# Linear attention and a SwiGLU block in one kernel: one more turn by DMA, wider slots, an earlier q load, and four banks for the last y

**Chip, cores, metric.** One core of one Trainium2 chip. The metric is the device time of one launch in microseconds (us). The device time is about 1.8 us longer than the span that the profile shows. Positions such as 36.29 are us from the start of the span.

## The reference, cut to what matters

```
k_proj = einsum('ks,bhsd->bhkd', E, k);  v_proj = einsum('ks,bhsd->bhkd', F, v)
attn   = softmax(q @ k_proj^T / 8)                 # 8 batches, 8 heads, 1024 tokens, 64 x 64
x      = (attn @ v_proj), heads side by side       # 8192 tokens x 512
g = x @ w_gate;  val = x @ w_val                   # 512 -> 1536
out = (g * sigmoid(g) * val) @ w_out               # 1536 -> 512, float32
```

## The kernel before

The kernel walks over 16 chunks of 512 tokens (two per batch) and, in each, over 12 blocks of 128 features. A block is four gate matmuls (`gps`), four value matmuls (`vps`) and, for the chunk before, four matmuls of the output (`yps`), each 512 columns wide. The attention of later tokens is placed between them in numbered slots: slot 2t lies between gate and value of block t, slot 2t+1 after value and output. The attention of one quarter of a half batch is called a unit: q is turned (`u_T`: four TensorE transposes, then a copy from PSUM), scores and exponential follow (`u_S`), then row sums (`u_R`, VectorE), normalisation (`u_N`, GpSimd), the turn of the attention (`u_A`: four transposes and a copy), and the product with v (`u_PV`, copied to xT, which the next chunk's matmuls read). In the profile `qTp`, `sc`, `aTp` and `pv` are the four results in PSUM, and `qT`, `ee` (the exponential), `AT` and `xT` what is made of them in SBUF; `qTd` and `AAd` belong to the turns by DMA.

```python
def u_T(b, u, at="a", eng=nc.scalar):          # turn of q by TensorE
    ps = bank(at, [P, 4, P], BF16, "qTp")
    for n in range(4):
        nc.tensor.transpose(out=ps[:, n, :], in_=..., identity=ident_bf[:])
    copy(eng, t[:], ps[:])                     # 128 x 512 bf16
def u_TD(b, ch):                               # the same for half a batch by DMA
    nc.sync.dma_start_transpose(out=t[:], in_=qb[b, ch]...)
def u_A(b, u, eng=nc.vector): ...              # turn of attention by TensorE; u_AD by DMA
def u_PV(b, ch, pr, eng=nc.scalar): ...        # one 512-column matmul, copied to xT
# (cut)
def f_y(c, n):
    if part == 0:
        if c == B * CH - 1 and i % 2: yy[c] = ps_g.tile(...)   # a gps bank
        else:                         yy[c] = ps_y.tile(...)   # the one y bank
    # 4 of 12 accumulating matmuls; after the last: ScalarE copy, store from SyncE's queue
# (cut) batch 0, second half
for i, u in enumerate(range(4, 8)):
    put(14+i, u_T, 0, u); put(15+i, u_S, 0, u); put(16+i, u_R, 0, u)
    put(16+i, u_N, 0, u); put(19+i, u_A, 0, u)
put(22, u_PV, 0, 1, 0); put(22, u_PV, 0, 1, 1); put(23, u_PV, 0, 1, 2); put(23, u_PV, 0, 1, 3)
```

Batches 2 to 7 are turned by DMA, batches 0 and 1 by TensorE. The products, turns and scores share three PSUM banks.

The softmax here doesn't subtract the row's maximum and nothing guards it: scores larger than these inputs give would overflow.

Of the kernel before, what the change touches and what calls it, by code (L numbers as in the profile page):

```python
# [9 lines left out]
AF = mybir.ActivationFunctionType  # L10
# [3 lines left out]
FP32 = mybir.dt.float32  # L14

B = 8
H = 8
S = 1024
D = 64
KP = 64  # L20
DM = H * D
DFF = 1536
P = 128
NJ = S // P
NPAIR = H // 2
NKT = DM // P
NFT = DFF // P
CH = 2
CW = 512
NIT = B * CH * NFT  # L30
BY_DMA = range(2, B)


@with_exitstack
def kernel(
# [19 lines left out]
    nc = tc.nc  # L55
    scale = 1.0 / float(D) ** 0.5
# [9 lines left out]
    y_pool = ctx.enter_context(tc.tile_pool(name="ysb", bufs=3))  # L66
    ps_g = ctx.enter_context(tc.tile_pool(name="psg", bufs=2, space=bass.MemoryType.PSUM))
    ps_v = ctx.enter_context(tc.tile_pool(name="psv", bufs=2, space=bass.MemoryType.PSUM))
    ps_y = ctx.enter_context(tc.tile_pool(name="psy", bufs=1, space=bass.MemoryType.PSUM))
# [11 lines left out]
    wo = w_pool.tile([P, NFT, DM], BF16, name="wo")  # L81
# [20 lines left out]
    def load_q(b, ch, parts=1):  # L102
        t = q_pool.tile([P, H, 4, D], BF16, name="qb", tag="qb")
        qb[b, ch] = t
        n = H // parts
        for i in range(parts):
            nc.gpsimd.dma_start(
                out=t[:, i * n : (i + 1) * n].rearrange("p h j d -> p h (j d)"),
                in_=q[b, i * n : (i + 1) * n].rearrange("h (p c j) d -> p c h (j d)", c=2, j=4)[:, ch],
            )  # L110

    def load_w_gv(c0, c1, which=(0, 1)):
        cs = slice(c0 * P, c1 * P)
        for wsrc, wdst in [((moe_w_gate, wg), (moe_w_val, wv))[i] for i in which]:
            nc.gpsimd.dma_start(
                out=wdst[:, :, cs],
                in_=wsrc[:, cs].rearrange("(t p) c -> p t c", p=P),
            )
# [11 lines left out]
    def bank(where, shape, dt, name):  # L130
        pool, tag = banks[where]
        return pool.tile(shape, dt, name=name, tag=tag)
# [4 lines left out]
    def u_KV(b, what="kv", hs=(0, H), at="a"):  # L137

        key = (b, what)
        if key not in kvp:  # L140
            kvp[key] = bank(at, [P, H, D], FP32, "kvp")
        t = kvp[key]
        h0, h1 = hs
        todo = [x for x in (("k", 0, ET, kb), ("v", 64, FT, vb)) if x[0] in what]
        for j in range(NJ):
            for _, lo, w, src in todo:
                nc.tensor.matmul(  # L147
                    out=t[lo : lo + 64, h0:h1].rearrange("p h d -> p (h d)"),
                    lhsT=w[:, j, :],
                    rhs=src[b][:, h0:h1, j, :],  # L150
                    start=(j == 0),
                    stop=(j == NJ - 1),
                )
        if "k" in what:
            if (b, "s") not in kvp:
                kvp[b, "s"] = aw.tile([KP, H, D], BF16, name="ks", tag="ks")
            nc.scalar.copy(out=kvp[b, "s"][:, h0:h1], in_=t[0:64, h0:h1])  # L157
        if "v" in what:
            tv = t[64:128].rearrange("p (a c) d -> p a c d", c=2)
            ps = slice(h0 // 2, h1 // 2)  # L160
            eng = nc.vector if b else nc.scalar
            copy(eng, BDV[b % 2][0:64, ps, 0:64], tv[:, ps, 0, :])
            copy(eng, BDV[b % 2][64:128, ps, 64:128], tv[:, ps, 1, :])
        if h1 == H:
            kvp.pop(key)
# [52 lines left out]
    def u_S(b, u, at="a"):  # L218
        ch, w = divmod(u, 4)
        g, i = divmod(w, 2)  # L220
        ps = bank(at, [P, 4, P], FP32, "sc")
        if b in BY_DMA:
            t = qT[b, ch, "d"][:].rearrange("p (h i) t -> p i h t", i=2)[:, i, 4 * g : 4 * g + 4]
        else:
            t = qT.pop((b, u))
        for n in range(4):
            nc.tensor.matmul(  # L227
                out=ps[:, n, :], lhsT=t[:, n, :], rhs=BD[b % 2][:, 4 * g + n, :], start=True, stop=True
            )
        e = aw.tile([P, 4, 2, KP], FP32, name="ee", tag="ee", bufs=4)  # L230
        nc.scalar.activation(  # L231
            out=e[:].rearrange("p h j k -> p (h j k)"),
            in_=ps[:].rearrange("p a k -> p (a k)"),
            func=AF.Exp,
            scale=scale,
        )
        ee[b, u] = e
# [9 lines left out]
    def u_N(b, u):  # L247
        ch, w = divmod(u, 4)
        g, i = divmod(w, 2)
        if b in BY_DMA:  # L250
            if (b, ch, "d") not in AA:
                AA[b, ch, "d"] = aw.tile([P, 4, H, KP], BF16, name="AAd", tag="AAd")
            a = AA[b, ch, "d"][:, 2 * i : 2 * i + 2, 4 * g : 4 * g + 4, :]
        else:
            a = AA[b, u] = aw.tile([P, 2, 4, KP], BF16, name="AA", tag="AA", bufs=4)
            a = a[:]
        eng = nc.vector if b == 0 and u in (2, 3) else nc.gpsimd
        eng.tensor_tensor(  # L258
            out=a.rearrange("p j h k -> p h j k"),
            in0=ee.pop((b, u))[:],  # L260
            in1=rr.pop((b, u))[:].unsqueeze(3).to_broadcast([P, 4, 2, KP]),
            op=ALU.mult,
        )
# [84 lines left out]
    yy = {}  # L348

    def f_y(c, n):  # L350
        i, part = divmod(n, 3)
        if part == 0:
            if c == B * CH - 1 and i % 2:
                yy[c] = ps_g.tile([P, DM], FP32, name="yps", tag="gps")
            else:
                yy[c] = ps_y.tile([P, DM], FP32, name="yps", tag="yps")
        for f in range(4 * part, 4 * part + 4):
            nc.tensor.matmul(  # L358
                out=yy[c][:],
                lhsT=hT[c][:, f, i * P : (i + 1) * P],  # L360
                rhs=wo[:, f, :],
                start=(f == 0),
                stop=(f == NFT - 1),
            )
        if part == 2:
            ysb = y_pool.tile([P, DM], FP32, name="ysb", tag="ysb")
            nc.scalar.activation(out=ysb[:], in_=yy.pop(c)[:], func=AF.Copy, scale=0.5)  # L367
            b, ch = divmod(c, CH)
            nc.sync.dma_start(
                out=out[b * S : (b + 1) * S, :].rearrange("(p j) c -> p j c", j=NJ)[:, 4 * ch + i, :],  # L370
                in_=ysb[:],
            )


    slots = defaultdict(list)
# [1 line left out]
    def put(s, fn, *a):  # L377
        slots[s].append((fn, a))

    def place(b):  # L380
        s0 = 48 * (b - 1)
        if b == 1:
            put(34, u_KV, 1, "k")
            put(36, u_KT, 1)
            put(41, u_KV, 1, "v")
            tt = (36, 37, 38, 39, 48, 50, 52, 54)
            sa = (37, 38, 39, 40, 49, 51, 53, 55)
            ta = (42, 43, 44, 45, 54, 56, 58, 60)
            sp = (45, 46, 46, 47, 62, 63, 64, 65)
        else:  # L390
            put(s0, u_KV, b)
            put(s0 + 3, u_KT, b)
            o = 14 if b == 2 else 6
            put(s0 + (3 if b == 2 else -6), u_TD, b, 0)
            put(s0 + (5 if b == 2 else -4), u_TD, b, 1)
            sa = [s0 + o + 3 * j for j in range(NJ)]
            put(sa[3] + 4, u_AD, b, 0)
            put(sa[7] + 4, u_AD, b, 1)
            sp = [s0 + i for i in (39, 41, 43, 45, 57, 59, 61, 63)]
        for j in range(NJ):  # L400
            if b not in BY_DMA:
                put(tt[j], u_T, b, j)
                put(ta[j], u_A, b, j)
            put(sa[j], u_S, b, j)
            put(sa[j] + 1, u_R, b, j)
            put(sa[j] + 1, u_N, b, j)
        for i in range(8):
            put(sp[i], u_PV, b, i // 4, i % 4)

    def run_slot(s):  # L410
        for fn, a in slots.pop(s, ()):
            fn(*a)

    with tc.manual_schedule():
# [74 lines left out]
        u_A(0, 2, nc.scalar)  # L489
        u_KV(0, "v", (4, 8), at="y")  # L490
        load_w_gv(4, 6, (1,))
        load_w_gv(6, 8)
        load_q(0, 1)
        load_w_gv(8, 10)
        load_w_gv(10, 12)
        load_wo(0)
# [12 lines left out]
        f_mm(0, 1, 1, 0)  # L509

        for i, u in enumerate(range(4, 8)):
            put(14 + i, u_T, 0, u)
            put(15 + i, u_S, 0, u)
            put(16 + i, u_R, 0, u)
            put(16 + i, u_N, 0, u)
            put(19 + i, u_A, 0, u)
        put(22, u_PV, 0, 1, 0)
        put(22, u_PV, 0, 1, 1)
        put(23, u_PV, 0, 1, 2)
        put(23, u_PV, 0, 1, 3)  # L520
# [3 lines left out]
        for b in range(1, B):  # L524
            place(b)
# [12 lines left out]
        for c in range(B * CH - 1):  # L538
            for n in range(NFT):
                f = n if c else 4 + (2 * n + 1) // 3  # L540
                ypart[(c + 1) * NFT + f].append((c, n))

        for t in range(NIT):
            c, f = divmod(t, NFT)
            i = 1 if t < 2 else None
# [3 lines left out]
            for a in ypart.pop(t, ()):  # L549
                f_y(*a)  # L550
            run_slot(2 * t + 1)
        for f in range(NFT):
            f_y(B * CH - 1, f)
        assert not slots and not ypart

# [28 lines left out]
```

## Time and profile before

| | before |
|---|---|
| time, median (lowest to highest) | 578.96 (578.88 to 580.07), 3 runs |
| span of the profiled run | 578.6 |
| TensorE / VectorE / ScalarE / GpSimd busy | 98% / 59% / 41% / 19% |
| granted TensorE clock | 1.0 |

The prediction below shows the busy row, the chain and the main waits. One more stretch is needed later, the end of batch 0's attention. This is the TensorE timeline of the kernel before: start, us, engine, line, operation, count, and in brackets the idle time that the profile admits.

```profile
45.93 1.03 PE L322 MATMUL gps<-xT,wg 128*128 128x512 bf16 x4
46.90 0.40 PE L274 MATMUL aTp<-ident_bf,AA 128*128 128x128 bf16 x4
47.13 0.38 PE L285 MATMUL pv<-AT,BDV 128*128 128x512 bf16 x1
47.72 0.38 PE L285 MATMUL pv<-AT,BDV 128*128 128x512 bf16 x1 [0.21 <-DVE AT L135]
...
49.23 1.49 PE L322 MATMUL gps<-xT,wg 128*128 128x512 bf16 x4
50.55 1.02 PE L322 MATMUL vps<-xT,wv 128*128 128x512 bf16 x4
```

Read it by starts. Four 512-column matmuls need 0.865 us, so 46.90 is 0.10 late. One needs 0.216, so 47.72 is 0.37 late, of which the bracket admits 0.21. The group at 49.23 took 1.32 us to the next start, 0.45 too long, and the bracket says nothing at all.

### The profile page before, as it was taken

The numbers are of one execution on the slowest core, as the hardware profiler recorded it, in microseconds if no ns is written. First come the engines' busy times: TensorE is split into PE (matmuls) and PEld (weight loads), VectorE is DVE, ScalarE is ACT, GpSimd is POOL, SyncE is SP. The second block draws the span as 40 slices with busy tenths as digits, with TensorE's granted clock in tenths as the row PEclk, the third lists the DMA queues.
The fourth block names the chain that finished last, engine by engine and source line by source line (L and its number), as shares of the span: only waits on it lengthen the run. The fifth ranks groups of instructions, "written<-read, shape, count | busy, mean of one in ns | idle before, by whom it ended". The sixth has DMA issues, their size and how long they took to land.

```text
span 578.6 us, 7968 instructions
## 1 busy us (share of the span) xinstructions
PE 567.8 (98%) x2987; PEld 268.7 (46%) x2987; DVE 340.4 (59%) x588; ACT 236.8 (41%) x415; POOL 107.9 (19%) x121
## 2 busy tenths in 40 slices
PE   8899999999999999999999999999999999999997
PEld 4644444544444444444444444444444444444443
DVE  2787555766556654666556655567546665545550
ACT  2654434443435434354334434354343543443321
POOL 6634031124002310025001330023200220000000
PEclk9999999999999999999999999999999999999999
DMA  9999962209940599027950299305991112101002
GB/s 160 195 201 198 207 103 65 74 24 189 175 104 19 105 194 175 18 68 113 186 128 36 56 167 185 70 34 87 192 177 37 48 45 73 37 36 37 27 29 91
DMA packets 101623, 60.29 MB, mean 104 GB/s; under 512 B 53840, under 2 KB 93264, under 8 KB 101584
## 3 DMA queue, kind: packets, MB, share of 16 engines
q0 software_dynamic: 42288, 29.89, 35.7%
q1 hardware_dynamic: 59296, 29.89, 23.6%
q8 instruction: 23, 0.38, 0.3%
q14 instruction: 16, 0.13, 0.1%
HBM read 60.29 MB, written 16.78 MB: 133 GB/s over the span
## 4 chain that ended last, share of the span: by engine, by line
PE 93%; DMA 2%; DVE 2%; ACT 1%; POOL 1%; issue 0%; POOLq 0%; DVEq 0%; ACTq 0%
PE yps L358 29%; PE vps L322 28%; PE gps L322 28%; PE kvp L147 3%; DMA vb<-in_v_dram 2%; PE sc L227 2%; PE pv L285 2%; DVE hT L346 1%; DVE s L341 0%; PE aTp L274 0%; DVE zz L242 0%; ACT ysb L367 0%; PE qTp L193 0%; ACT qT L135 0%; POOL kb L88 0%
## 5 line engine op out<-in xcount | busy, mean ns | idle before, releaser
L341 DVE SCALAR_TENSOR_TENSOR s<-th,gps 128x512 f32<-128x512 f32 x192 | 130.5, 680 | 133.7 <-ACT th L334 133.5
L322 PE MATMUL gps<-xT,wg 128*128 128x512 bf16 (+1 forms) x776 | 198.1, 377 | 0.5 <-ACT xT L135 0.3
L322 PE MATMUL vps<-xT,wv 128*128 128x512 bf16 (+1 forms) x776 | 197.5, 377 | 0.0
L358 PE MATMUL yps<-wo,hT 128*128 128x512 bf16 x768 | 194.6, 379 | 0.7 <-ACT ysb L367 0.7
L334 ACT ACTIVATE th<-gps 128x512 f32<-128x512 f32 x192 | 114.7, 597 | 165.1 <-PE gps L322 162.2
L346 DVE TENSOR_TENSOR hT<-s,vps 128x512 bf16<-128x512 f32 x192 | 132.0, 687 | 22.9 <-PE vps L322 2.5
L358 PEld LDWEIGHTS <-hT 128*128 128x128 bf16 x768 | 75.1, 98 | 91.5 <-issue 1.0
L322 PEld LDWEIGHTS <-wv 128*128 128x128 bf16 x776 | 73.7, 98 | 82.6 <-issue 3.8
L322 PEld LDWEIGHTS <-wg 128*128 128x128 bf16 x776 | 73.8, 98 | 81.1 <-issue 1.0
L258 POOL TENSOR_TENSOR AAd<-ee,rr 128x512 bf16<-128x512 f32 x48 | 49.9, 1040 | 300.6 <-issue 165.8
L367 ACT ACTIVATE ysb<-yps 128x512 f32<-128x512 f32 x64 | 38.2, 597 | 79.3 <-PE yps L358 79.3
L135 ACT CAST xT<-pv 128x512 bf16<-128x512 f32 x62 | 36.0, 584 | 51.2 <-PE pv L285 50.2
L242 DVE TENSOR_REDUCE zz<-ee 128x8 f32<-128x512 f32 x64 | 43.5, 680 | 20.4 <-ACT ee L231 20.2
L231 ACT ACTIVATE ee<-sc 128x512 f32<-128x512 f32 x64 | 38.0, 597 | 20.7 <-PE sc L227 20.7
L258 POOL TENSOR_TENSOR AA<-ee,rr 128x512 bf16<-128x512 f32 x14 | 14.5, 1040 | 59.0 <-DVE rr L244 21.9
L285 PE MATMUL pv<-AT,BDV 128*128 128x512 bf16 x60 | 22.4, 379 | 0.2 <-DVE AT L135 0.2
L227 PEld LDWEIGHTS <-qTd 128*128 128x128 bf16 x192 | 14.8, 98 | 11.3
L135 DVE CAST BDV<-kvp 64x256 bf16<-64x256 f32 x14 | 6.0, 427 | 22.1 <-ACT ks L157 20.0
L227 PE MATMUL sc<-BD,qTd 128*128 128x128 bf16 x192 | 18.6, 219 | 0.0
L244 DVE RECIPROCAL rr<-zz 128x8 f32<-128x8 f32 x64 | 13.0, 203 | 6.2
L147 PE MATMUL kvp<-kb,ET 128*64 128x512 bf16 (+1 forms) x72 | 15.5, 357 | 1.2 <-DMA kb<-in_k_dram 1.2
L147 PE MATMUL kvp<-vb,FT 128*64 128x512 bf16 (+1 forms) x72 | 15.5, 358 | 1.0 <-DMA vb<-in_v_dram 1.0
(49 smaller groups left out, 156.4 us busy)
## 6 DMA issues: line engine op xcount, KB each, us to landing
out_dram<-ysb SPq DMA_DIRECT2D x64, 256.0 KB, 2.4
qb<-in_q_dram POOLq DMA_DIRECT2D x15, 512.0 KB, 17.0
kb<-in_k_dram POOLq DMA_DIRECT2D x7, 1024.0 KB, 11.3
vb<-in_v_dram POOLq DMA_DIRECT2D x7, 1024.0 KB, 13.5
wo<-in_moe_w_out_dram POOLq DMA_DIRECT2D x2, 768.0 KB, 15.4
wg<-in_moe_w_gate_dram POOLq DMA_DIRECT2D x5, 256.0 KB, 11.4
wv<-in_moe_w_val_dram POOLq DMA_DIRECT2D x5, 256.0 KB, 11.5
kb<-in_k_dram POOLq DMA_DIRECT2D x2, 512.0 KB, 8.7
```

The source lines that it names most:

```text
L135: (nc.scalar.copy if eng is nc.scalar else eng.tensor_copy)(out=out, in_=in_)
L147: nc.tensor.matmul(out=t[lo : lo + 64, h0:h1].rearrange("p h d -> p (h d)"), lhsT=w[:, j, :], rhs=src[b][:, h0:h1, j, :], start=(j == 0), ...
L227: nc.tensor.matmul(out=ps[:, n, :], lhsT=t[:, n, :], rhs=BD[b % 2][:, 4 * g + n, :], start=True, stop=True)
L231: nc.scalar.activation(out=e[:].rearrange("p h j k -> p (h j k)"), in_=ps[:].rearrange("p a k -> p (a k)"), func=AF.Exp, scale=scale,)
L242: nc.vector.reduce_sum(out=z[:], in_=e[:], axis=AX.X)
L258: eng.tensor_tensor(out=a.rearrange("p j h k -> p h j k"), in0=ee.pop((b, u))[:], in1=rr.pop((b, u))[:].unsqueeze(3).to_broadcast([P, 4, 2 ...
L322: nc.tensor.matmul(out=ps[:, ts], lhsT=(wg, wv)[w][:, kt, f * P : (f + 1) * P], rhs=x[:, kt, ts], start=(kt == 0), stop=(kt == NKT - 1),)
L334: nc.scalar.activation(out=th[:], in_=ps[:], func=AF.Tanh, scale=0.5)
L341: nc.vector.scalar_tensor_tensor(out=s1[:], in0=th[:], scalar=1.0, in1=g[:], op0=ALU.add, op1=ALU.mult)
L346: nc.vector.tensor_tensor(out=hT[c][:, f, :], in0=s1[:], in1=ps[:], op=ALU.mult)
L358: nc.tensor.matmul(out=yy[c][:], lhsT=hT[c][:, f, i * P : (i + 1) * P], rhs=wo[:, f, :], start=(f == 0), stop=(f == NFT - 1),)
L367: nc.scalar.activation(out=ysb[:], in_=yy.pop(c)[:], func=AF.Copy, scale=0.5)
```

## The change

Its intent: take more transposes off TensorE, and let no TensorE instruction wait for a copy that could have been earlier.

(The diff is shortened; loops and calls are abridged.)

```diff
-BY_DMA = range(2, B)
+BY_DMA = [(b, ch) for b in range(1, B) for ch in range(CH)][1:]   # batch 1's second half too
 # batch 1
+put(30, u_TD, 1, 1)
-put(41, u_KV, 1, "v")
+put(40, u_KV, 1, "v")
-tt = (36, 37, 38, 39, 48, 50, 52, 54)      # turns of q
-sa = (37, 38, 39, 40, 49, 51, 53, 55)      # scores
-ta = (42, 43, 44, 45, 54, 56, 58, 60)      # turns of attention
-sp = (45, 46, 46, 47, 62, 63, 64, 65)      # products
+sa = (37, 38, 39, 40, 48, 50, 52, 54)
+tt = (35, 36, 37, 38)
+ta = (41, 42, 43, 44)
+put(57, u_AD, 1, 1)
+sp = (43, 44, 45, 46, 66, 67, 68, 69)
 # loads
+load_q(0, 1)
 load_w_gv(6, 8)
-load_q(0, 1)
 # batch 0, second half
-put(14 + i, u_T, 0, u); put(15 + i, u_S, 0, u); put(16 + i, u_R / u_N, 0, u); put(19 + i, u_A, 0, u)
-put(22, u_PV, 0, 1, 0)
+put(12 + i, u_T, 0, u); put(14 + i, u_S, 0, u); put(15 + i, u_R / u_N, 0, u); put(19 + i, u_A, 0, u, nc.scalar)
+put(21, u_PV, 0, 1, 0)
 # last chunk's y
-    y bank and gps bank in turn, four tiles of 512 columns
+    yy[c] = bank("gvgv"[i] if c == B * CH - 1 else "y", ...)      # tiles 0 to 2
+def f_y_last(c, i):                                               # tile 3
+    for cs, where in ((slice(0, 320), "v"), (slice(320, DM), "g")):
+        ...                      # 12 matmuls, eviction, store issued by ScalarE
```

More of the change, by code (lines that the diff above doesn't have):

```diff
@@ L221, in u_S @@
         ps = bank(at, [P, 4, P], FP32, "sc")
-        if b in BY_DMA:
+        if (b, ch) in BY_DMA:
             t = qT[b, ch, "d"][:].rearrange("p (h i) t -> p i h t", i=2)[:, i, 4 * g : 4 * g + 4]
@@ L249, in u_N @@
         g, i = divmod(w, 2)
-        if b in BY_DMA:
+        if (b, ch) in BY_DMA:
             if (b, ch, "d") not in AA:
@@ L352, in f_y, with y_mm @@
         if part == 0:
-            if c == B * CH - 1 and i % 2:
-                yy[c] = ps_g.tile([P, DM], FP32, name="yps", tag="gps")
-            else:
-                yy[c] = ps_y.tile([P, DM], FP32, name="yps", tag="yps")
-        for f in range(4 * part, 4 * part + 4):
+            yy[c] = bank("gvgv"[i] if c == B * CH - 1 else "y", [P, DM], FP32, "yps")
+        y_mm(c, i, range(4 * part, 4 * part + 4), slice(0, DM))
+        if part == 2:
+            y_out(c, i, slice(0, DM), nc.sync)
+    def y_mm(c, i, fs, cs):
+        for f in fs:
             nc.tensor.matmul(
-                out=yy[c][:],
+                out=yy[c][:, cs],
                 lhsT=hT[c][:, f, i * P : (i + 1) * P],
-                rhs=wo[:, f, :],
+                rhs=wo[:, f, cs],
                 start=(f == 0),
@@ L364, in f_y, with y_out @@
             )
-        if part == 2:
-            ysb = y_pool.tile([P, DM], FP32, name="ysb", tag="ysb")
-            nc.scalar.activation(out=ysb[:], in_=yy.pop(c)[:], func=AF.Copy, scale=0.5)
-            b, ch = divmod(c, CH)
-            nc.sync.dma_start(
-                out=out[b * S : (b + 1) * S, :].rearrange("(p j) c -> p j c", j=NJ)[:, 4 * ch + i, :],
-                in_=ysb[:],
-            )
+    def y_out(c, i, cs, eng):
+        ysb = y_pool.tile([P, DM], FP32, name="ysb", tag="ysb")
+        nc.scalar.activation(out=ysb[:, cs], in_=yy[c][:, cs], func=AF.Copy, scale=0.5)
+        b, ch = divmod(c, CH)
+        eng.dma_start(
+            out=out[b * S : (b + 1) * S, :].rearrange("(p j) c -> p j c", j=NJ)[:, 4 * ch + i, cs],
+            in_=ysb[:, cs],
+        )
+    def f_y_last(c, i):
+        for cs, where in ((slice(0, 320), "v"), (slice(320, DM), "g")):
+            yy[c] = bank(where, [P, DM], FP32, "yps")
+            y_mm(c, i, range(NFT), cs)
+            y_out(c, i, cs, nc.scalar)
     slots = defaultdict(list)
@@ L400, in place @@
         for j in range(NJ):
-            if b not in BY_DMA:
+            if (b, j // 4) not in BY_DMA:
                 put(tt[j], u_T, b, j)
@@ L511 @@
         for i, u in enumerate(range(4, 8)):
-            put(14 + i, u_T, 0, u)
-            put(15 + i, u_S, 0, u)
-            put(16 + i, u_R, 0, u)
-            put(16 + i, u_N, 0, u)
-            put(19 + i, u_A, 0, u)
-        put(22, u_PV, 0, 1, 0)
+            put(12 + i, u_T, 0, u)
+            put(14 + i, u_S, 0, u)
+            put(15 + i, u_R, 0, u)
+            put(15 + i, u_N, 0, u)
+            put(19 + i, u_A, 0, u, nc.scalar)
+        put(21, u_PV, 0, 1, 0)
         put(22, u_PV, 0, 1, 1)
@@ L551 @@
             run_slot(2 * t + 1)
-        for f in range(NFT):
-            f_y(B * CH - 1, f)
+        for n in range(9):
+            f_y(B * CH - 1, n)
+        f_y_last(B * CH - 1, 3)
         assert not slots and not ypart
```

## The prediction

> **What bounds the kernel now.** I began with the page: the busy row and the chain that ended last.
>
> ```profile
> PE 567.8 (98%) x2987; PEld 268.7 (46%) x2987; DVE 340.4 (59%) x588; ACT 236.8 (41%) x415; POOL 107.9 (19%) x121
> ...
> PE 93%; DMA 2%; DVE 2%; ACT 1%; POOL 1%; issue 0%; POOLq 0%; DVEq 0%; ACTq 0%
> ```
>
> TensorE carries 93% of the chain, the clock row reads 9 throughout, and no other engine is above 59%. So two things can save time: TensorE work that disappears, and moments in which TensorE stands. The group rows with shapes kept apart give the size of the first:
>
> ```profile
> L274 PE MATMUL aTp<-ident_bf,AA 128*128 128x128 bf16 x64 | 6.2, 219 | 0.2 <-DVE AA L258 0.2
> L193 PE MATMUL qTp<-ident_bf,qb 128*128 128x128 bf16 x64 | 6.0, 219 | 0.4 <-DMA qb<-in_q_dram 0.4
> ```
>
> The mean of 219 ns is one matmul's pass from start to modelled end; passes overlap, so it isn't what one costs. The wait table gives TensorE only some 6 us in all, because an overlapping modelled end hides part of a stall. I therefore read the TensorE timeline by starts. An undisturbed group of four 512-column matmuls starts 0.865 us before the next group (28.52, 29.39, 30.25 in this timeline), and four 128-column ones take 0.225 us. Whatever exceeds that is a stall. The first batch's second half:
>
> ```profile
> 36.29 0.39 PE L193 MATMUL qTp<-ident_bf,qb 128*128 128x128 bf16 x4
> 36.52 1.03 PE L322 MATMUL vps<-xT,wv 128*128 128x512 bf16 x4
> 37.62 0.40 PE L227 MATMUL sc<-BD,qT 128*128 128x128 bf16 x4
> 37.86 0.39 PE L193 MATMUL qTp<-ident_bf,qb 128*128 128x128 bf16 x4
> 38.08 1.03 PE L322 MATMUL gps<-xT,wg 128*128 128x512 bf16 x4
> ```
>
> The vps group at 36.52 should be over at 37.38, and the scores start at 37.62: 0.24 us lost. The turn at 36.29 is copied by ScalarE at 36.99 for 0.58 us, that is until 37.57, so the scores waited for that copy although the wait table shows next to none of it. The second batch shows the same, and so does the end of its first half, where the next chunk's matmuls wait for the last xT copy:
>
> ```profile
> 72.83 1.03 PE L322 MATMUL gps<-xT,wg 128*128 128x512 bf16 x4
> 74.20 0.40 PE L227 MATMUL sc<-BD,qT 128*128 128x128 bf16 x4 [0.35 <-ACT qT L135]
> ...
> 89.37 0.81 PE L322 MATMUL gps<-xT,wg 128*128 128x512 bf16 x3
> 90.47 0.38 PE L322 MATMUL gps<-xT,wg 128*128 128x512 bf16 x1 [0.30 <-ACT xT L135]
> ```
>
> These are 74.20 - 72.83 - 0.865 = 0.50 us and 90.47 - 89.37 - 3 x 0.216 = 0.45 us. Last, the end, from the timeline of all engines:
>
> ```profile
> 562.38 1.03 PE L358 MATMUL yps<-wo,hT 128*128 128x512 bf16 x4
> ...
> 563.45 0.60 ACT L367 ACTIVATE ysb<-yps 128x512 f32<-128x512 f32 x1 [1.13 <-PE yps L358]
> ...
> 564.10 10.52 PE L358 MATMUL yps<-wo,hT 128*128 128x512 bf16 x48 [0.69 <-ACT ysb L367]
> ...
> 574.70 0.60 ACT L367 ACTIVATE ysb<-yps 128x512 f32<-128x512 f32 x1 [1.99 <-PE yps L358]
> ```
>
> The 48 matmuls of the last chunk start when ScalarE has emptied the one y bank (564.05). They could start at 562.38 + 0.865 = 563.25. After the last matmul only one full-width eviction, one store (issued 575.33, landed 2.0 us later) and 1.3 us of closing remain up to 578.6.
>
> **What the Trainium skill says.** "TensorE: Matmul & The Clock Gate", Wait - 56ns, not 53.3ns?, puts a warm start-to-start at N/2.4 GHz plus about 2.5 ns. The trace agrees: 0.225/4 = 56 ns at 128 columns, 0.865/4 = 216 ns at 512. "Perfetto Trace Analysis", Tensor Engine Instruction, says that TensorE's end times are a model; that is why I count starts. The same page, Matmuls, says independent matmul groups should rotate through different PSUM banks so that evacuation overlaps the next group's matmuls; the single y bank at 564 breaks that and the trace charges 0.85 us. "DMA: Bandwidth & Descriptors", Issuing engines are not separate DMA queues, says all issuers share 16 DMA engines: the new turns compete with the loads. The trace shows that too: one attention turn issued at 130.9, while the next batch loads, took 18.0 us to land against a median of 8.7.
>
> **The change part by part.**
>
> *Second batch's second half by DMA.* It removes 16 q transposes and 16 attention transposes: 8 groups x 0.225 = **1.80 us** of TensorE path, confirmed by the instruction order (40 rows fewer: 64 for these transposes and their weight loads, less 24 for the last y's split). Four ScalarE copies (0.58 each) and four VectorE copies (0.42) go as well, beside the path. Added are two DMA turns. The q turn can issue when its load lands (48.58 + 14.5 = 63.1) and is needed near 87; even 18 us leaves time. The attention turn follows the last normalisation at slot 55, about 104, and its product moved from slots 62-65 to 66-69, about 115; the DMA share at 105 to 120 is 0.14, so I expect a landing near the smallest seen, 4.3. Both hidden.
>
> *Two slots between turn and scores.* First batch: the stalls before its four scores are 0.24, 0.30, 0.24, 0.30 = 1.08 us, by starts. Second batch: 0.30 (at 69.33) and 0.50 = **0.80 us**. With a group of 0.865 more between, against a need of 0.70 (turn start to copy start) + 0.58, they vanish.
>
> *First batch's turns back and products.* In the kernel before, 0.10 us is lost before the last attention transpose (46.90), 0.37 at the second product (47.72), 0.45 in the first gps group of the next chunk (49.23 to 50.55), 0.92 in all. The new order gives these copies to ScalarE, 0.58 instead of 0.42. Laying its queue out by hand from 42.4 on, with 0.54 to 0.58 per operation: in about 3.0 us of TensorE time it has three attention copies, four xT copies and a tanh to do, 4.3 us or more, with a lead of about 0.5. I get 0.3 us lost before the third product and about 0.5 for the last xT copy, 0.8 in all. Net with the scores: 1.08 + 0.92 - 0.80 = **1.20 us**.
>
> *Second batch's first half one slot earlier.* The product for the last xT part comes a slot earlier, and the 0.45 us at 90.47 goes: **0.45 us**.
>
> *q's second half ahead of the fourth weights.* The landings of the kernel before, from each issue and its time to landing: third value weights 29.3, fourth gate weights 30.6, fourth value weights 31.9, q 34.6 (2.7 after the one before). Reordered: q 32.0, gate 33.3, value 34.6. First uses: gate 33.70, q's turn 34.57, value 34.79. Everything arrives, by as little as 0.2 us. I charge **-0.05 us** for the risk.
>
> *Last y in four banks.* The start at 564.10 moves to 563.25: **0.85 us**. VectorE's last hT of 563.83 is used only by the twelfth matmul, 2.4 us later, so it does not bind. The last tile in 320 and 192 columns has the same columns and 12 more matmuls: 12 x 2.5 ns = 0.03 lost. The eviction of 192 columns instead of 512: from 597 ns at 512 and about 370 at 256, a slope of 0.88 ns gives 0.32, a gain of 0.28. The final store has 98 KB instead of 256; I estimate 0.2 saved of its 2.0 us. The first part's eviction (0.43) and issue (0.33, taken from the SyncE queue) fit in the 12 x 82.5 ns = 0.99 us of the second part's matmuls. Net **0.45 us**.
>
> Sum: 1.80 + 1.20 + 0.80 + 0.45 - 0.05 + 0.85 + 0.45 = 5.50. Then 578.96 - 5.5 = **573.5 us**, 0.95% less.
>
> **The rivals.** *ScalarE becomes the wait in the first batch.* It then carries turns, exponentials, attention copies and products' copies between about 42 and 48. For it: the queue count above; against it: the same copies leave VectorE, which was late there too (two copies at 47.25). If all stalls merely move, the 1.20 shrinks to nothing: 574.7. *The fourth weights come late.* For it: 0.2 us of slack worked out from landings, at a DMA busy share above 1 in the early windows; against it: only one transfer's order changes. Cost if it happens 0.3 to 0.8: about 574. *The DMA turns come late or hold up others.* The SyncE queue runs in order, so a blocked turn holds back the y stores behind it, and three y buffers could run out. A late attention turn would stop the product at slot 66. For it: the 18 us landing; against it: the low DMA share there. Cost 1 to 3 us: 575 to 576. *The transposes were free.* If TensorE had waited then anyway, removing them would gain nothing: 575.3. Against it: in the stretch from 90.7 to 113 all groups follow each other at full rate but for 0.09 us at changes of tile shape.
>
> **Range and chances.** The transposes, the second-batch stalls and the y bank (3.9 us with 0.45 for xT) are read directly. The first batch (0.4 to 2.0), weights and tail carry the doubt, and a surprise of DMA is likelier to cost than gain. I take 572.4 to 575.0. A 2% gain would need 567.4, over twice the sum of all; a 2% loss needs a failure of 17 us. So faster 0.02, same 0.97, slower 0.01.
>
> **What would show it.** Right: 32 TensorE transposes fewer; starts before the first two batches' scores with no gap above 0.05; some wait for ScalarE's xT or AT copies left near 46 to 48; the last chunk's matmuls starting straight after the previous group, three full-width evictions, then 320 and 192 columns; a span of about 573.2. Wrong: a TensorE wait on DMA for weights near 34, a score or product of the second batch waiting for a DMA turn, a ScalarE issue that holds up the 192-column eviction, or a time above 575.

## The result, and the profile after

The changed kernel takes **573.9 us** (572.65 to 574.16, 4 runs) against 579.13 (578.88 to 580.07, 4 runs) for the one before: ratio 0.9903, 95% interval 0.9884 to 0.9921. Ratios here are the mean time of one kernel's fast runs over that of the other's in the same rounds, so not quite the ratio of the medians. In later rounds the same kernel gave 573.45 against 579.15, ratio 0.9895 (0.988 to 0.991).

The page of the changed kernel, busy row and chain:

```profile
PE 561.2 (98%) x2910; PEld 268.6 (47%) x2967; DVE 336.8 (59%) x580; ACT 237.0 (41%) x416; POOL 107.9 (19%) x121
...
PE 94%; DMA 2%; POOL 1%; ACT 1%; issue 1%; DVE 0%; POOLq 0%
```

TensorE bounds it as before, and the span is 572.4 against 578.6. A difference of medians of 5.2 us beside one of spans of 6.2 us asks for an explanation, so I cut each trace at the same instructions, by starts:

| stretch | before | before, again | changed | changed, again |
|---|---|---|---|---|
| start to first gps matmul (opening) | 22.48 | 21.88 | 22.57 | 21.82 |
| to gps of chunk 0's seventh block | 11.22 | 11.22 | 11.22 | 11.22 |
| to first vps of chunk 1 (batch 0's second half) | 16.85 | 16.84 | 15.26 | 15.26 |
| to first gps of chunk 2 (batch 1's first half) | 38.82 | 38.82 | 37.98 | 37.98 |
| to first gps of chunk 3 (batch 1's second half) | 38.26 | 38.26 | 36.01 | 36.01 |
| to last vps of chunk 15 | 433.90 | 433.90 | 433.90 | 433.90 |
| to last eviction | 13.18 | 13.18 | 12.32 | 12.32 |
| to end | 3.94 | 3.94 | 3.14 | 3.14 |

Every stretch after the opening repeats to 0.01 us. The opening, which waits for the first loads, lay between 21.1 and 22.7 us in the 14 traces, with the same TensorE instructions, and the later stretches don't move with it. So I compare stretches, and use times only to see that they agree. The stretches after the opening differ by 1.59 + 0.84 + 2.25 + 0.86 + 0.80 = **6.34 us**, inside the intervals of both ratios (0.988 to 0.991 of 579.15 us is 5.2 to 6.9 us less).

Batch 0's second half in the changed trace. First the turns and scores, as in the prediction's third fence:

```profile
36.82 0.39 PE L227 MATMUL sc<-BD,qT 128*128 128x128 bf16 x4
37.05 0.39 PE L193 MATMUL qTp<-ident_bf,qb 128*128 128x128 bf16 x4
37.27 1.03 PE L322 MATMUL vps<-xT,wv 128*128 128x512 bf16 x4
38.13 0.39 PE L227 MATMUL sc<-BD,qT 128*128 128x128 bf16 x4
```

From 37.27 to 38.13 is 0.86: no stall before the scores. Then the end of that stretch:

```profile
46.41 1.03 PE L322 MATMUL vps<-xT,wv 128*128 128x512 bf16 x4
47.29 0.59 PE L285 MATMUL pv<-AT,BDV 128*128 128x512 bf16 x2
47.72 1.48 PE L322 MATMUL gps<-xT,wg 128*128 128x512 bf16 x4
49.04 1.02 PE L322 MATMUL vps<-xT,wv 128*128 128x512 bf16 x4
```

The third product at 47.29 follows 46.41 by 0.88, so it waits 0.01 and not the 0.3 that I had laid out. The gps group still takes 1.32 to the next start, 0.45 too long, exactly as before the change. I had laid such a wait to ScalarE, so here is its queue (changed kernel, ScalarE's timeline):

```profile
45.56 0.59 ACT L135 CAST xT<-pv 128x512 bf16<-128x512 f32 x1
46.17 0.60 ACT L334 ACTIVATE th<-gps 128x512 f32<-128x512 f32 x1
46.66 0.58 ACT L135 COPY AT<-aTp 128x512 bf16<-128x512 bf16 x1
47.13 1.65 ACT L135 CAST xT<-pv 128x512 bf16<-128x512 f32 x3
```

It works almost without a gap from 45.56 to 48.78, and the third and fourth matmuls of the gps group need the last two of these copies. The operations start only 0.47 to 0.49 apart where they touch (46.17, 46.66, 47.13), though each lasts 0.58 to 0.60. That is why the attention copy was done at 47.24, in time for the third product. But the full queue is not what costs the 0.45 us. The third product starts at 47.29, and its xT copy, the second of the three in the last line, starts at 47.70, 0.41 us later. In the kernel before, ScalarE stood idle at this place and the copy came just as long after its product, at 49.21 after 48.79:

```profile
49.21 1.07 ACT L135 CAST xT<-pv 128x512 bf16<-128x512 f32 x2 [0.49 <-PE pv L285]
```

Both times the copies of the last two products follow these products directly, 0.48 to 0.49 us apart, and the gps group waits for them. So the wait comes from the slot of the last two products, just ahead of that group. Two experiments below agree: four copies fewer on ScalarE leave the 0.45 us, products one slot earlier remove it.

The DMA turns, from the SyncE queue of the changed kernel:

```profile
62.12 7.33 SPq L205 DMA_TRANSPOSE qTd<-qb  x1
...
103.24 1.77 SPq L212 DMA_TRANSPOSE AT<-AAd  x1
```

The q turn landed 13.0 us after its issue, at 75.1, and its first scores come at 87.89. The attention turn landed 4.3 us after its issue, at 107.5, and its first product comes at 114.82. Both had room to spare. The issue of the q turn held the queue for 7.3 us, so that a y store whose tile was ready at 63.9 went out at 69.50; it cost TensorE nothing, for without this turn (first experiment) the stretch is no shorter: 38.21 with one more transpose group in it, against 37.98. The end, all engines:

```profile
557.80 11.42 PE L360 MATMUL yps<-wo,hT 128*128 128x512 bf16 x63
...
568.31 0.44 ACT L370 ACTIVATE ysb<-yps 128x320 f32<-128x320 f32 x1 [1.03 <-PE yps L360]
568.78 0.37 ACTq L372 DMA_DIRECT2D out_dram<-ysb  x1
569.26 0.33 ACT L370 ACTIVATE ysb<-yps 128x192 f32<-128x192 f32 x1 [0.51 <-PE yps L360]
```

The last chunk's matmuls follow the previous group in one piece. The first part's store is issued and ScalarE is free again before the second part is complete.

### The profile page after: what moved, and what is told of

It is laid out like the page before. It is cut to its first block, busy times and chain, and to the rows that moved or that the text cites. A ratio compares the mean times of both kernels' runs of the same rounds, so it can differ in the third digit from the quotient of the medians.

```text
span 572.4 us, 7867 instructions
## 1 busy us (share of the span) xinstructions
PE 561.2 (98%) x2910; PEld 268.6 (47%) x2967; DVE 336.8 (59%) x580; ACT 237.0 (41%) x416; POOL 107.9 (19%) x121
## 4 chain that ended last, share of the span: by engine, by line
PE 94%; DMA 2%; POOL 1%; ACT 1%; issue 1%; DVE 0%; POOLq 0%
PE yps L360 29%; PE vps L322 29%; PE gps L322 29%; PE kvp L147 3%; PE sc L227 2%; DMA vb<-in_v_dram 2%; PE pv L285 2%; PE aTp L274 0%; ACT xT L135 0%; PE qTp L193 0%; POOL kb L88 0%; PE kTp L172 0%; POOL qb L107 0%; ACT th L334 0%; PE pv L300 0%
## 5 line engine op out<-in xcount | busy, mean ns | idle before, releaser
L322 PE MATMUL gps<-xT,wg 128*128 128x512 bf16 (+1 forms) x755 | 195.7, 377 | 1.2
L360 PE MATMUL yps<-wo,hT 128*128 128x512 bf16 (+2 forms) x761 | 191.5, 376 | 0.8
L258 POOL TENSOR_TENSOR AAd<-ee,rr 128x512 bf16<-128x512 f32 x52 | 54.1, 1040 | 319.5 <-issue 168.4
L370 ACT ACTIVATE ysb<-yps 128x512 f32<-128x512 f32 (+1 forms) x65 | 38.4, 590 | 78.1 <-PE yps L360 74.4
L227 PEld LDWEIGHTS <-qTd 128*128 128x128 bf16 x208 | 16.0, 98 | 12.3
L227 PE MATMUL sc<-BD,qTd 128*128 128x128 bf16 x208 | 20.1, 219 | 0.1
L258 POOL TENSOR_TENSOR AA<-ee,rr 128x512 bf16<-128x512 f32 x10 | 10.3, 1038 | 35.2 <-DVE rr L244 33.6
## 6 DMA issues: line engine op xcount, KB each, us to landing
kb<-in_k_dram POOLq DMA_DIRECT2D x7, 1024.0 KB, 11.6
wo<-in_moe_w_out_dram POOLq DMA_DIRECT2D x2, 768.0 KB, 14.8
wg<-in_moe_w_gate_dram POOLq DMA_DIRECT2D x5, 256.0 KB, 10.4
wv<-in_moe_w_val_dram POOLq DMA_DIRECT2D x5, 256.0 KB, 10.4
```

The source lines that it names most:

```text
L227: nc.tensor.matmul(out=ps[:, n, :], lhsT=t[:, n, :], rhs=BD[b % 2][:, 4 * g + n, :], start=True, stop=True)
L258: eng.tensor_tensor(out=a.rearrange("p j h k -> p h j k"), in0=ee.pop((b, u))[:], in1=rr.pop((b, u))[:].unsqueeze(3).to_broadcast([P, 4, 2 ...
L322: nc.tensor.matmul(out=ps[:, ts], lhsT=(wg, wv)[w][:, kt, f * P : (f + 1) * P], rhs=x[:, kt, ts], start=(kt == 0), stop=(kt == NKT - 1),)
L360: nc.tensor.matmul(out=yy[c][:, cs], lhsT=hT[c][:, f, i * P : (i + 1) * P], rhs=wo[:, f, cs], start=(f == 0), stop=(f == NFT - 1),)
L370: nc.scalar.activation(out=ysb[:, cs], in_=yy[c][:, cs], func=AF.Copy, scale=0.5)
```

## The experiments

Theory: TensorE sets the end, so each transpose off it and each start that no longer waits is worth just what the starts show. Rivals: the transposes or stalls were free, or the stalls only move to another engine; the DMA turns, the q order or ScalarE's store cost or gain something that I have not counted. Ten variants ran, and the two kernels once more; all gave correct results.

**Batch 1's second half back on TensorE.**

```diff
-BY_DMA = [(b, ch) for b in range(1, B) for ch in range(CH)][1:]
+BY_DMA = [(b, ch) for b in range(2, B) for ch in range(CH)]
-put(30, u_TD, 1, 1) ... put(57, u_AD, 1, 1)
+tt = (35, 36, 37, 38, 46, 48, 50, 52);  ta = (41, 42, 43, 44, 54, 56, 58, 60)
```

> The changed kernel with one part undone: the second batch's second half is turned by TensorE again (two slots between turn and scores kept). Theory (TensorE bounds, so each removed group of four 128-column transposes is worth its 0.225 us): 8 groups, 1.80 us slower than the changed kernel, that is about 4.4 us faster than before by trace span, and the stretch from the second group of matmuls of chunk 1 (49.04 in the changed trace) to the first gps group of chunk 3 grows by 1.8 us. Rival (the transposes stood where TensorE would have waited anyway): no more than 0.3 us slower. Rival (DMA turns held something up): faster than the changed kernel.

The two stretches became 38.21 (one turn now lies in it) and 37.57: 0.23 + 1.56 = 1.79 us more; time 575.42 (ratio 0.9925). Eight groups at 0.225 are 1.80. The transposes were not free, and their price is their start-to-start time.

**Batch 0's second half as before** (one slot between turn and scores, attention copies on VectorE).

```diff
-put(12+i, u_T ..); put(14+i, u_S ..); put(15+i, u_R, u_N ..); put(19+i, u_A, 0, u, nc.scalar); put(21, u_PV, 0, 1, 0)
+put(14+i, u_T ..); put(15+i, u_S ..); put(16+i, u_R, u_N ..); put(19+i, u_A, 0, u);            put(22, u_PV, 0, 1, 0)
```

> The changed kernel with the first batch's second half placed as before: one slot between turn and scores, attention copies on VectorE. Theory: the 1.55 us of stalls read by starts (1.08 before four scores, 0.10 before the last attention transpose, 0.37 before the second product) come back, and the 0.45 us in the first gps group of chunk 1 stays: 1.5 us slower. Rival (the stalls only move to ScalarE's queue): less than 0.5 us slower.

The stretch is 16.84, the value before; every later one that the edit does not touch is unchanged but for 0.22 us in the long one. There a DMA turn was late: batch 2's first attention turn, issued at 127.24, landed at 145.71, 18.5 us later, and its product started at 145.76 in place of 145.55. The changed kernel's own trace has 1.1 us to spare at this turn (143.52 against 144.65), another trace 0.1. Time 575.25 (0.9927). The stalls do not move; they come from this placement.

**The last y as before.**

```diff
-yy[c] = bank("gvgv"[i] if c == B * CH - 1 else "y", ...)
+yy[c] = bank("g" if c == B * CH - 1 and i % 2 else "y", ...)
-f_y_last(B * CH - 1, 3)
+for n in range(9, 12): f_y(B * CH - 1, n)
```

> The changed kernel with the last chunk's y as before: one y bank and one gps bank in turn, last tile whole, stored from the SyncE queue. Theory: the last chunk's matmuls wait 0.85 us for ScalarE again, and the tail from the start of the last eviction to the end grows from 3.14 to 3.9 us: 1.6 us slower in all. Rival (VectorE's last hT or the closing sets the end): less than 0.5 us slower.

The two last stretches were 13.18 and 3.79, so 0.86 + 0.65 = 1.51 us more; time 575.19 (0.9924). The wait for the one y bank returned.

**q's second half behind the fourth weights.**

```diff
-load_q(0, 1); load_w_gv(6, 8)
+load_w_gv(6, 8); load_q(0, 1)
```

> The changed kernel with q's second half behind the fourth weights again, its turns still at the early slots. Theory: q then lands at about 34.6, when the first turn would start (34.65), so TensorE waits there for q, 0.1 to 0.5 us; nothing else changes: 0.1 to 0.5 us slower. Rival (the order is without effect): no wait on q, same within 0.1 us. Rival (the reorder cost weights): faster than the changed kernel.

The stretch is 15.26, no wait for q; time 573.43 (0.9894). q was issued at 23.04 and landed 10.4 later, at 33.45, and the first turn started at 34.22. My expectation was wrong by a microsecond, because I took the landing from another trace with a later issue. The order gained nothing here; I can't exclude that it helps in a run with a slower opening.

**Four banks, but the last tile whole.**

```diff
-for n in range(9): f_y(B * CH - 1, n)
-f_y_last(B * CH - 1, 3)
+for n in range(12): f_y(B * CH - 1, n)
```

> The changed kernel with four banks for the last y, but the last tile whole (512 columns, one eviction, one store on the SyncE queue). Tells the bank's share of the end from the split's. Theory: the 0.85 us of the bank stay won (last chunk's matmuls follow straight on, 12.3 us from the last vps group to the last eviction), and the time from the start of the last eviction to the end is as in the kernel before, 3.85 to 3.95 us in place of 3.0 to 3.35: 0.7 us slower than the changed kernel. Rival (the split is worth nothing, ScalarE's issue eats it): within 0.2 us of it.

12.34 to the last eviction, so the bank's gain is kept; 3.78 from there to the end; time 574.35 (0.9899). The bank and the split are separate gains. In the traces the last stretch is 3.78 to 3.94 with a whole tile (four traces) and 3.12 to 3.32 split (ten traces).

**Both parts stored from the SyncE queue.**

```diff
-y_out(c, i, cs, nc.scalar)
+y_out(c, i, cs, nc.sync)
```

> The changed kernel with both parts of the last tile stored from the SyncE queue in place of ScalarE's. Theory (the gain of the split is the shorter eviction and the smaller store): last eviction to the end within 0.1 us of the changed kernel's 3.0 to 3.35. Rival (the queue makes the difference, since ScalarE needs no message to SyncE and its store is issued at once): 0.2 to 0.4 us more.

3.12, and 573.24 (0.9887). The queue makes no difference. The last eviction takes 0.33 in place of 0.60, and the last store lands 1.7 us after its issue in place of 2.0; both come from the smaller part.

**Attention copies of batch 0 on VectorE, at the new slots.**

```diff
-put(19 + i, u_A, 0, u, nc.scalar)
+put(19 + i, u_A, 0, u)
```

> The changed kernel with the four attention copies of the first batch's second half on VectorE again, at the new slots. Read in the stretch from the gps group of the seventh feature block (33.79 in the changed trace) to the first vps group of chunk 1 (49.04): 15.26 us there, 16.85 before. Theory (ScalarE's queue makes the 0.45 us wait in chunk 1's first gps group): ScalarE has 4 x 0.58 us less to do, the last xT copy comes earlier and the stretch is 14.8 to 15.1. Rival (VectorE is as late, and the products wait for its copies): 15.3 or more, with a wait before a product.

The rival was right. The stretch is 16.28, and the TensorE timeline of this kernel shows where:

```profile
43.18 0.39 PE L274 MATMUL aTp<-ident_bf,AA 128*128 128x128 bf16 x4
44.45 0.38 PE L285 MATMUL pv<-AT,BDV 128*128 128x512 bf16 x1 [0.89 <-DVE AT L135]
```

The product waits 1.05 us by starts for a VectorE copy that is queued behind row sums and the block's own work. The 0.45 us in the gps group stays as well, although ScalarE has four copies fewer and stood idle for 0.45 us before the third xT copy: its queue isn't the cause. So giving these copies to the slower engine (0.58 instead of 0.42) is worth 1.02 us of the 1.59. The time, 574.01 in 2 runs, hardly shows it: this trace has the shortest opening of all, 21.09.

**Batch 0's second half one slot earlier throughout.**

```diff
-put(12+i, u_T ..); put(14+i, u_S ..); put(15+i, u_R, u_N ..); put(19+i, u_A, ..)
-put(21, u_PV, 0, 1, 0); put(22, u_PV, 0, 1, 1); put(23, u_PV, 0, 1, 2); put(23, u_PV, 0, 1, 3)
+put(11+i, u_T ..); put(13+i, u_S ..); put(14+i, u_R, u_N ..); put(18+i, u_A, ..)
+put(20, u_PV, 0, 1, 0); put(21, u_PV, 0, 1, 1); put(22, u_PV, 0, 1, 2); put(22, u_PV, 0, 1, 3)
```

> The changed kernel with the first batch's whole second half one slot earlier (turns from slot 11, the last two products in slot 22). Theory (only the late xT copy is left there; q landed at 31.0 and the first turn starts at 33.8): the 0.45 us goes and the same stretch falls from 15.26 to 14.8 us, with 0.4 us of time. Rival (the chain of scores, VectorE and GpSimd cannot follow): a new wait before an attention transpose or a product, and 15.2 or more. Rival (q not landed): a wait for q before the first turn.

The stretch is 14.54. One turn (0.22) now lies ahead of its first landmark, so the fair sum is from the first gps matmul on: 11.44 + 14.54 = 25.98 against 26.48, 0.50 us less. The end of it, TensorE's timeline:

```profile
47.78 1.03 PE L322 MATMUL gps<-xT,wg 128*128 128x512 bf16 x4
48.65 1.03 PE L322 MATMUL vps<-xT,wv 128*128 128x512 bf16 x4
```

47.78 to 48.65 is 0.87: with the last two products a slot earlier, the wait for the last xT copy is gone. Time 573.08, ratio 0.988 (0.9864 to 0.9897). By stretches this is the best version that ran, though its trace gives half of the gain back in the long stretch: 0.26 us, again batch 2's first attention turn, which took 18.5 us to land. By time it can't be told apart from the changed kernel (0.9895, 0.988 to 0.991, in other rounds), and the two never ran in the same rounds.

**The two kernels once more.**

> The kernel before once more, for a second trace of it. The first trace pair differs by 6.2 us of span, the medians by 5.2 us. Theory (only the opening, up to the first gps matmul, differs from run to run; 21.1 to 22.7 us so far): every later stretch repeats within 0.05 us, 16.85, 38.82, 38.26, 433.90 and 13.18 us, and the span follows the opening. Rival (the stalls of before that I read by starts are chance): a stretch differs by 0.3 us or more.

> The changed kernel once more, on the same chip and in the same rounds as the two that are meant to beat it. Theory: 15.26, 37.98, 36.01, 433.90 and 12.32 us again, 5 to 6 us faster than before in these rounds.

The stretches repeat, as the table above shows, and the openings differ; 579.83 (one run) and 573.45. The stalls are properties of the order of instructions. Within the nine runs of the kernel before in these rounds the span alone ranged from 577.1 to 578.7, about what the opening varies.

**Batch 1's first half by DMA as well**, in the hope of another 1.80 us.

```diff
-BY_DMA = [...][1:]
+BY_DMA = [(b, ch) for b in range(1, B) for ch in range(CH)]
+put(28, u_TD, 1, 0); put(43, u_AD, 1, 0)
-put(34, u_KV, 1, "k"); put(36, u_KT, 1)
+put(32, u_KV, 1, "k"); put(35, u_KT, 1)
-sa = (37, 38, 39, 40, ...); sp = (43, 44, 45, 46, ...)
+sa = (38, 39, 40, 41, ...); sp = (45, 46, 46, 47, ...)
```

> The changed kernel with the second batch's first half turned by DMA as well: its last 8 groups of TensorE transposes go, scores one slot later, products two slots later. Theory (a transpose group is worth 0.225 us wherever the turn lands in time): 1.8 us faster than the changed kernel, the stretch from chunk 1's first vps group to chunk 2's first gps group 36.2 in place of 37.98, if the q turn lands before about 66 and the attention turn, issued at about 75, before about 81. Rival (the DMA turns compete with the third batch's loads, which run until about 74; one turn took 13 us there): TensorE waits for qTd or AT 1 to 8 us, and the kernel is no faster or slower.

588.22 us, ratio 1.0154: 14.8 us slower than the changed kernel in the same rounds. The rival was right that TensorE waits for both turns, and the loss is greater than these waits. TensorE's wait table, then its timeline:

```profile
PE pv L285 <- DMA AT<-AAd: 6.2, 1, 6.2
PE sc L227 <- DMA qTd<-qb: 5.5, 1, 5.5
```

```profile
65.71 1.03 PE L322 MATMUL gps<-xT,wg 128*128 128x512 bf16 x4
72.21 0.61 PE L227 MATMUL sc<-BD,qTd 128*128 128x128 bf16 x4 [5.48 <-DMA qTd<-qb]
72.61 1.91 PE L322 MATMUL vps<-xT,wv 128*128 128x512 bf16 x4
74.32 3.62 PE L360 MATMUL yps<-wo,hT 128*128 128x512 bf16 x8
77.73 0.44 PE L227 MATMUL sc<-BD,qTd 128*128 128x128 bf16 x4
```

The q turn, issued at 54.0, took 18.1 us to land, beside the loads of this batch and the next. From 72.61 to 74.32 the vps group needs 1.71 us in place of 0.865. The stretches of 1 us with busy time per engine, granted clock (the number after the POOL column), DMA share (the time of all packets over the 16 DMA engines, which can exceed 1) and GB/s say why:

```profile
70.00:71.00 1.00, 0.00 (x0) 0.00 (x0) 0.00 (x0) 0.00 (x0) 0.00 (x0) 1.00 1.23 196
71.00:72.00 1.00, 0.00 (x0) 0.00 (x0) 0.00 (x0) 0.00 (x0) 0.00 (x0) 0.51 1.25 197
...
76.00:77.00 1.00, 1.00 (x4) 0.42 (x3) 0.16 (x1) 0.00 (x0) 0.69 (x1) 0.50 1.35 110
77.00:78.00 1.00, 1.00 (x7) 0.45 (x6) 0.00 (x0) 0.02 (x1) 1.00 (x2) 0.58 1.25 68
78.00:79.00 1.00, 1.00 (x9) 0.34 (x6) 0.00 (x0) 1.00 (x2) 0.24 (x1) 1.00 1.29 72
```

The clock is halved during the wait and stays so for about 5.6 us after work resumes. The sum, by starts: waits 72.21 - 65.71 - 0.865 = 5.64 and, for the attention turn (groups at 88.18 and 95.40), 6.35; half speed 2.70 after the first and 1.43 after the second; less 1.80 for the transposes: 14.3 us, and the stretch grew from 37.98 to 52.39, 14.4.

The second wait is only in part a matter of traffic, the cause that the rival names. The attention turn was issued at 88.40, when the fourth normalisation had ended (88.37), and its product was due at 88.18 + 0.865 = 89.05. It landed after 7.0 us, beside a q load; the fastest turn in any trace, 4.2 us, would have been some 3.6 us late too. My expectation of an issue at 75 was a misreading: in the changed kernel the fourth normalisation of the same half batch ends at 79.74. That products further back would have saved this wait was not tried.

**Both, with batch 0 one slot earlier.**

> The two together: second batch wholly by DMA and the first batch's second half one slot earlier. Theory: both add, 2.2 us faster than the changed kernel if the turns land in time. Rival: as for the kernel with both halves by DMA alone, then only the 0.45 us are left.

587.89 us, ratio 1.0137; the rival again: 14.54 for batch 0, but 51.23 for batch 1, waits of 4.9 and 6.3 us by starts.

## Why the prediction was right, and where its terms were off

The predicted 573.5 lies 0.4 us from the measured 573.9, which is inside the stated 572.4 to 575.0, and the parts that were undone alone each lost about what they had won. But the closeness is partly luck: the sum was 5.50 us and the stretches, free of the opening, show 6.34. Term by term:

- *Transposes, 1.80*: undone alone, 1.79. Right, also that both DMA turns were hidden; the margins were 12.8 and 7.3 us.
- *Second batch, 0.80 for the scores and 0.45 for xT*: 0.84, and 2.25 - 1.80 = 0.45. Right. I did not undo these two apart from the rest; they are read in the stretches.
- *First batch, 1.20*: 1.59. Mis-sized. The stalls of 1.08 + 0.10 + 0.37 went entirely. I let ScalarE's queue lose 0.8 us, and it lost nothing. The 0.3 before the third product did not come, because I queued ScalarE's operations 0.54 to 0.58 apart where they run 0.47 to 0.49 apart. A wait of 0.45 for the last xT copy came where I had 0.5, but for another reason than mine: it is the wait of the kernel before, set by the slot of the last two products. That this size fitted is luck. I also took the move of the copies to ScalarE for a burden. Undone alone, VectorE costs 1.02 us more: it, not ScalarE, would have been the late engine.
- *q's order, -0.05 for the risk*: 0. The weights came in time, and without the new order q would have come in time too.
- *Four banks, 0.85*: 0.86. Right.
- *Split of the last tile, 0.45*: 0.80 against the kernel before, 0.64 when undone alone. Mis-sized. The eviction gained 0.27, as laid out; the store and closing gained 0.37 to 0.53 and not the 0.2 that I estimated. The store's landing accounts for some 0.34 of it (2.02 to 1.68).

The missed terms add up to 0.39 + 0.35 + 0.05 + 0.04 = 0.83, and 5.50 + 0.83 is 6.33 us. That the medians differ by only 5.2 us in the first rounds, and 5.7 in the last, fits the openings, which vary by up to 1.6 us; which opening a run without a trace had is not known.

Of the rivals, that stalls merely move was refuted by undoing the placement, and that the transposes were free by putting them back. The late DMA turn did not happen here, but it is real: with one half batch more by DMA it costs 14.4 us. What separates the two cases is the time between a turn's issue and its first use. A low DMA share, my reason against it, helped the attention turn only. The moved q turn ran at a DMA share of 1.25 (60 to 75, changed kernel), took 13.0 us and had 25.8. In the other kernel the q turn ran at 1.20, took 18.1 and had 12.5. The moved attention turn took 4.3 us and had 11.6; the other took 7.0 and had 0.65.

## What to carry to other kernels

When one engine is 98% busy, read its timeline from start to start against the undisturbed rate: stalls of 0.1 to 0.5 us stand there that idle columns hide, and each can be priced before the change and checked after, in stretches that here repeat to 0.01 us. Ask of each whether the copying engine was busy or itself waiting: in the first case another engine helped here, in the second only moving the product did. Choose the engine of a copy by who is free at that moment, not by whose copy is shorter. Move a turn to DMA only where its landing under the loads of that moment, here 4 to 18 us, still leaves room, because a long TensorE wait is paid again in clock.

## What the Trainium skill lacked or had wrong

- "TensorE: Matmul & The Clock Gate", Part 4: PE-mode transpose, gives a duration of about 275 ns for a 128 x 128 transpose in a kernel's context and says the fast clock does not engage for it. The same duration is 219 ns in the profile here (its end is modelled), at a granted clock of 1.0. The page doesn't say what a transpose costs in a stream: 32 of them, put back among matmuls, cost 1.79 us, 56 ns each.
- The same page, Back-to-back issue gap, gives about 81 ns at 128 columns and about 131 ns at 512 for a stream in which every matmul has its own weight load. Such a stream runs here at 56 and 216 ns.
- The same page, What's actually happening, puts both the fall and the return of the clock at one window of about 3.4 us or more, idle or busy. Where both halves of batch 1 went by DMA, the clock came back about 5.6 us after work resumed from the first wait (72.21 to some 77.8) and about 2.9 us after the second (95.40 to 98.3). It fell at 71.0, about 4.3 us after TensorE's last busy moment (66.7), and at 91.5, about 2.3 us after it (89.2). So the shorter figure of each pair is below the page's 3.4.
- "DMA: Bandwidth & Descriptors", Latency and other measured facts, has a bandwidth for DMA transposes but no time to landing beside other traffic. A half batch's turn landed in 4.2 to 18.5 us after its issue, the longest at a DMA share of 1.24.
